# Attention scores as plain float32 products of four heads on their own 32 rows

## Chip, cores and metric

The kernel runs on one core of a Trainium2 chip, in one launch. The metric is the device time of that core in microseconds. A profile is one execution taken by the hardware profiler; its span runs from the first to the last instruction.

## What is computed

The input is one sequence of 2048 tokens of width 448, with 16 heads of 28. Two attention layers run on the same tokens and a gate mixes them. Layer A is a linear attention with learned feature maps; layer B is full softmax attention, and the change lies in B.

```python
# layer B, per head, Dh = 28
scores = einsum("bhqd,bhkd->bhqk", q, k) * Dh ** -0.5
p = softmax(scores, axis=-1)
o = einsum("bhqk,bhkd->bhqd", p, v)
b = merge_heads(o) @ wo
# x = A_x for both layers
g = sigmoid((x * gate_w).sum(-1, keepdims=True))
out = g * a + (1 - g) * b
```

## The kernel before

**Stages.** The kernel first makes the projections (q and k of layer B go through `keep_qk` to a scratch tensor `qk_d` in HBM), then layer A, then the values of layer B, and from about a third of the time on the attention of B, step by step. The orders on TensorE (PE), VectorE (DVE), ScalarE (ACT) and GpSimd (POOL) are those written in the code. The order of the DMAs on the SP queue is laid out by the framework, and each DMA waits for the one eight before it besides its own data.

**Two floats for one.** A float32r product is one TensorE instruction and keeps fewer bits than float32. `keep_qk` therefore writes a pair for each q and k: index 0 the rounded value, made by ACT (L571), and index 1 the remainder, made by DVE from the first (L572). A score tile stacks them on the rows of the array: `load_stack` puts four blocks of 28 rows into 128 partitions, q as (high, high, low, low), k as (high, low, high, low), so that one float32r product over 128 rows gives the whole score. Each tile holds four heads side by side in its free dimension.

**The maximum.** The exponential needs a maximum for each query. Row 0 of the key stack holds -1 and row 0 of the query stack holds the query's maximum, so the subtraction is done within the product. The maxima are found ahead by visits (`mx_visit`): four heads at a time, each a float32r product of its 28 rows of high parts in its own 32 rows of the array (`tile_position=(32 * j, 0)`), written to four PSUM banks. ACT copies one of the four out (`rl`, L325), DVE reduces the others (L329, L332, L335). A finished maximum lies in `nm`, and `load_nm` copies it into row 0 of the query stack by DMA.

**The attention.** There are 4 groups of four heads, 4 blocks of 512 queries, and 16 tiles of 128 keys: 256 steps `s`. Each step issues, in this order, the scores of step s for four heads (`scores`, L850, tiles `st`), the values of step s-1 (`values`, L977, four heads in four column tiles of 32, plain float32, accumulated in `pv`), and, in the first 212 steps, one visit (L321, tiles `pm`). ACT makes four exponentials a step (L868, `p<-st`), then `rl`. At the end of a query block `finish` normalizes; with the last group of heads an output projection (`project`, L988) falls into four steps of a block.

**The PSUM banks.** Seven banks rotate through a list `free`, an eighth holds `pv`. `scores` takes four from the head of the list. After both halves of the scores the list is laid out anew, `a` being the four score banks of this step and `m` the three that the last visit held for DVE:

```python
free.extend([a[0], m[0], a[1], m[1], a[2], a[3], m[2]] if m else a)
```

`mx_banks` then takes the first four of them, gives the first (the one that `rl` reads) back to the end of the list at once, and holds the other three. So in a step with a visit the four score banks are, in the order of the heads: two read by the last exponentials of the step before, one read by DVE in an earlier visit, and the one read by `rl` of the visit before. When the visits are over, six banks rotate and one is kept for the projections.

**The stacks.** There are two query stacks `qst` and five key stacks `kst`, 128 x 4 x 512 each, cleared by POOL before the attention starts (L817, L819). The last block's earlier heads (`load_out`) are loaded into a key stack that is no longer used.

Of the kernel before, what the change touches and what calls it, by code (L numbers as in the profile page):

```python
# [8 lines left out]
F32 = mybir.dt.float32  # L9
F32R = mybir.dt.float32r  # L10
U32 = mybir.dt.uint32
AF = mybir.ActivationFunctionType
# [5 lines left out]
P = 128  # L18
# [3 lines left out]
DH = 28  # L22
GW = 112
NG = 4
NT = S // P
NQ = S // 512
SCALE = DH ** -0.5
# [7 lines left out]
def f32(ap):  # L35
    return ap.bitcast(F32)
# [3 lines left out]
def gated_mix_kernel(ctx, tc, xT, wqkB, wvB, wvA, wkAT, wqAT, phi, woA, woB,  # L40
# [7 lines left out]
    nc = tc.nc  # L48
# [12 lines left out]
    def ps_s(nm):  # L61
        return ps.tile([P, 512], F32, tag="s", name=nm, bufs=psn[0])
# [13 lines left out]
    q_d = [qk_d[g * GW:(g + 1) * GW] for g in range(NG)]  # L76
    k_d = [qk_d[D + g * GW:D + (g + 1) * GW] for g in range(NG)]
# [40 lines left out]
    def tok_major(dst, t, w, n, mid=None):  # L118

        todo = [(x, w[:, i, b, :n]) for b, x, i in x3(slice(t * P, (t + 1) * P))]  # L120
        if mid is None:
            run(dst[:, :n], todo)
            return
        for i, (l, r) in enumerate(todo):
            mid(i)
            nc.tensor.matmul(dst[:, :n], l, r, start=i == 0, stop=i == len(todo) - 1,  # L126
                             skip_group_check=True)
# [36 lines left out]
    def take_acts():  # L164
        while acts:
            acts.pop(0)()
# [401 lines left out]
    def keep_qk(m, t, pq, ev):  # L568
        tt = slice(t * 512, (t + 1) * 512)
        e = ev.tile([P, 2, 512], F32R, tag="ev", name=f"ev{t}_{m}")  # L570
        nc.scalar.copy(e[:, 0, :], pq)  # L571
        nc.vector.tensor_sub(e[:, 1, :], pq, f32(e[:, 0, :]))  # L572
        nc.sync.dma_start(qk_d[m * P:(m + 1) * P, :, tt], f32(e))


# [115 lines left out]
    def value_b(t, mid=None):  # L691
        pv = ps_s(f"pvb{t}")
        tok_major(pv, t, wvB_s, D, mid)
        nc.scalar.copy(vb[t // 8][:, t % 8, :, 0:DH], pv[:, :D].rearrange("p (h d) -> p h d", d=DH))  # L694
# [11 lines left out]
    for i in range(2 * NT + 11):  # L706
        t, q = i, i - NT
# [31 lines left out]
        if 0 <= q < NT:  # L739
            pq = ps_s(f"pq{q}")  # L740
# [69 lines left out]
    at = ctx.enter_context(tc.tile_pool(name="at", bufs=1, side="right", reuse_waits="tile"))  # L810
    qst_of, kst_of = {}, {}
# [1 line left out]


    def stack(nm, keys):
        r = at.tile([P, 4, 512], F32R, name=nm)
        nc.gpsimd.memset(f32(r), 0.0)  # L817
        if keys:
            nc.gpsimd.memset(f32(r[0:1]), -1.0)  # L819
        return r  # L820

    def load_stack(r, src, c, parts):
        for b, i in enumerate(parts):
            nc.sync.dma_start(f32(r[32 * b + 4:32 * b + 32]),
                              src[:, i, c:c + 512].rearrange("(j d) n -> d j n", d=DH))
        return r

    def load_q(gq):
        g, qb = divmod(gq, NQ)
        qst_of[gq] = load_stack(qst[gq % 2], q_d[g], qb * 512, (0, 0, 1, 1))  # L830

    def load_nm(gq):
        nm = nm_of.pop(gq)
        row = f32(qst_of[gq][0:1].rearrange("p a (t b r) -> p (a t) b r", b=4, r=32))
        for b in range(4):
            nc.sync.dma_start(row[:, :, b, :], nm[32 * b:32 * b + 16, :])

    def load_k(g, kb):
        kst_of[(g, kb)] = load_stack(kst[(4 * g + kb) % 5], k_d[g], kb * 512, (0, 1, 0, 1))

    NS = NG * NQ * NT
    pv_of, pts, late, mids = {}, {}, {}, {}

    def scores(s, i):

        gq, kt = divmod(s, NT)
        g, qb = divmod(gq, NQ)

        def score(j, st):
            nc.tensor.matmul(st, kst_of[(g, kt // 4)][:, j, (kt % 4) * P:(kt % 4 + 1) * P],  # L850
                             qst_of[gq][:, j, :], start=True, stop=True)

        if s == 0:
            p = at.tile([P, 2, 512], F32, name=f"p{s}_{i}")
            st = ps_mx(f"st{s}_{i}", i)
            for jl in range(2):
                score(2 * i + jl, st[:, jl, :])
            nc.scalar.activation(p, st, AF.Exp, scale=SCALE)
            pts.setdefault(s, []).extend([p[:, 0, :], p[:, 1, :]])
            return  # L860
        sts = []
        for j in (2 * i, 2 * i + 1):
            used.append(free.pop(0))
            sts.append(bank(used[-1], f"st{s}_{j}"))
            score(j, sts[-1])
        for st in sts:
            p = late_p.tile([P, 512], F32, tag="p", name=f"p{s}_{len(pts.get(s, []))}", bufs=8)
            nc.scalar.activation(p, st, AF.Exp, scale=SCALE)  # L868
            pts.setdefault(s, []).append(p)
        if i == 1:  # L870
            a, m = used[:], held[:]
            free.extend([a[0], m[0], a[1], m[1], a[2], a[3], m[2]] if m else a)
            used.clear()
            held.clear()

    qst = [stack("qst0", False)]
    kst = [stack(f"kst{i}", True) for i in range(5)]
# [10 lines left out]
    for t in range(8, NT):  # L888


        if t < NT - 1:
            value_b(t, lambda i: mx_unit() if (11 * (t - 8) + i + 1) * rest // 77
                    > (11 * (t - 8) + i) * rest // 77 else None)
        else:
            value_b(t, lambda i: scores(0, i // 3 - 1) if i in (4, 7) else None)
        take_acts()
        if t in (8, 12):
            load_k(0, t // 12)
# [9 lines left out]
    free, used, held = list(range(7)), [], []  # L908
    spare = []

    def bank(i, nm):
        return ps2.tile([P, 512], F32, tag=f"g{i}", name=nm, bufs=1)
# [17 lines left out]
    def load_out(qb):  # L930


        if qb < NQ - 1:
            o = late_p.tile([P, NG - 1, 2, 512], F32R, tag="oL", name=f"oL{qb}", bufs=1)
            oL_of[qb] = [o[:, b] for b in range(NG - 1)]
        else:
            o = kst[(4 * NG) % 5]
            oL_of[qb] = [o[:, 0:2], o[:, 2:4],
                         late_p.tile([P, 2, 512], F32R, tag="oLl", name="oLl", bufs=1)]
        tt = slice(qb * 512, (qb + 1) * 512)  # L940
        for b in range(2):
            nc.sync.dma_start(f32(oL_of[qb][b]), o_d[b * P:(b + 1) * P, :, tt])
        r = oL_of[qb][2]
        for i in range(2):
            nc.sync.dma_start(f32(r[:80, i, :]), o_d[256:336, 0, tt])
        nc.sync.dma_start(f32(r[80:, 0, :]), o_d[288:336, 1, tt])
        nc.sync.dma_start(f32(r[80:96, 1, :]), o_d[288:304, 1, tt])
        nc.sync.dma_start(f32(r[96:, 1, :]), o_d[256:288, 1, tt])
# [145 lines left out]
    for s in range(NS + 16):  # L1094
        take_acts()
        if s < NS:
            gq, kt = divmod(s, NT)
            g, qb = divmod(gq, NQ)
            if s in (0, 3):
                load_k(0, 2 + s // 3)  # L1100
            if g + 1 < NG and qb == NQ - 1 and kt % 4 == 2:
                load_k(g + 1, kt // 4)
            if kt == 12 and gq + 1 < NG * NQ:
                load_q(gq + 1)
            if kt == (12 if gq + 1 < 14 else 14) and gq + 1 < NG * NQ - 1:
                load_nm(gq + 1)
            if s in OUTS:
                load_out(OUTS.index(s))
            if g == NG - 1 and kt == 8:
                load_acc(qb)  # L1110
            if s:
                scores(s, 0)
                scores(s, 1)
        if s == NS:
            tail_open()
            tail_fill(3)
        if 0 < s <= NS:
            values(s - 1)
            if s % NT == 0:
                finish(s // NT - 1, s)  # L1120
        if s:
            mx_visit()
        if mxs["f"] == len(flats):
            mx_fin()
        if s in mids:
            mids.pop(s)()
        if mxs["f"] == len(flats) and not spare:
            spare_open()
        if NG * NQ - 1 in nm_of and NG * NQ - 1 in qst_of:
            load_nm(NG * NQ - 1)  # L1130
        for fn in late.pop(s, []):
            fn()
# [68 lines left out]
```

## Time and profile before

| | |
|---|---|
| time, median of 2 runs | 1028.54 us (1028.19 to 1028.88) |
| span of the profiled execution | 1027.1 us |
| PE busy | 1018.7 us, 99% |
| ACT busy | 819.4 us, 80% |
| DVE busy | 672.8 us, 65% |
| POOL busy | 245.1 us, 24% |
| DMA | 98.88 MB, mean 96 GB/s |
| granted TensorE clock | 0.998 |

The profiled execution's own time is its span and what lies around it; the median of the runs is 1.4 us above the span. In the rows below, a line names engine, source line and operation, the tile written and the tiles read, then sizes and count. PE stands for matmuls, PEld for the weight loads ahead of them, SPq for the DMA issues. Groups show busy time, mean nanoseconds of one, then the idle time of the engine ahead of them and what ended it. A timeline row begins with the start and the length of the group in us. A row of the windows view has each engine's busy time and the number of its instructions in that stretch, in the order PE, PEld, DVE, ACT, POOL. Matmul ends are modelled, so starts are the better measure.

### The profile page before, as it was taken

The page shows a single profiled execution, that of the slowest core. Times are in us where ns is not written, and L with a number is a line of the kernel's source. Part 1 is how long each engine was busy: PE and PEld are TensorE (multiplying, and loading weights), DVE is VectorE, ACT ScalarE, POOL GpSimd, SP SyncE. Part 2 cuts the span into 40 slices and gives each one's busy share as a digit, 9 for nine tenths or more (in the row PEclk, how much of TensorE's full clock was granted, in tenths as well). Part 3 has the DMA queues.
Part 4 walks back from the last instruction along what each step waited for, and adds up shares of the span by engine and source line. Part 5 has one row for each costly group of instructions (what it writes and reads, how often), then busy time and mean ns, then how long its engine had stood idle before and what let it go on. Part 6 is the DMA issues. An engine that isn't in the chain of part 4 may idle for free.

```text
span 1027.1 us, 17751 instructions
## 1 busy us (share of the span) xinstructions
PE 1018.7 (99%) x6344; PEld 561.2 (55%) x6344; DVE 672.8 (65%) x1335; ACT 819.4 (80%) x1534; POOL 245.1 (24%) x213
## 2 busy tenths in 40 slices
PE   8999999999999999999999999999999999999998
PEld 7878888878779433333333333333333333354545
DVE  5466566997750578888878788787878887710102
ACT  5354445687753899999999999999999999969672
POOL 1226456688436302111011110101201101011010
PEclk9999999999999999999999999999999999999999
DMA  8873110132245703233633123522313355414311
GB/s 294 292 243 116 42 34 19 43 90 79 91 129 122 158 19 83 65 71 68 127 70 77 46 66 81 129 57 50 87 46 74 87 131 138 124 56 127 122 42 54
DMA packets 64025, 98.88 MB, mean 96 GB/s; under 512 B 17952, under 2 KB 24720, under 8 KB 63936
## 3 DMA queue, kind: packets, MB, share of 16 engines
q1 hardware_dynamic: 63936, 97.74, 35.4%
q8 instruction: 50, 0.82, 0.4%
q14 instruction: 39, 0.32, 0.1%
HBM read 69.54 MB, written 27.78 MB: 95 GB/s over the span
## 4 chain that ended last, share of the span: by engine, by line
PE 95%; DVE 2%; DMA 1%; ACT 1%; issue 0%; SPq 0%; DVEq 0%; ACTq 0%
PE st L850 29%; PE pv L977 25%; PE pm L321 9%; PE pqk L108 5%; PE poa L108 4%; PE pk L126 4%; PE pva L126 4%; PE pob L108 3%; PE pq L108 3%; PE pvb L108 2%; PE pmb L284 2%; PE pvb L126 2%; PE pn L532 1%; PE pft L520 1%; PE pkv L475 1%; PE poL L1011 1%
## 5 line engine op out<-in xcount | busy, mean ns | idle before, releaser
L868 ACT ACTIVATE p<-st 128x512 f32<-128x512 f32 x1020 | 525.9, 609 | 29.5 <-PE st L850 27.8
L332 DVE TENSOR_REDUCE part<-pm 128x1 f32<-128x512 f32 x477 | 304.6, 685 | 131.5 <-PE pm L321 124.9
L850 PE MATMUL st<-qst,kst 128*128 128x512 f32 x1024 | 315.6, 430 | 0.5 <-ACT vb L694 0.5
L977 PE MATMUL pv<-p,vb 128*32 128x512 f32 x2048 | 272.8, 605 | 0.2 <-DVE oUb L398 0.2
L850 PEld LDWEIGHTS st<-qst,kst 128*128 128x128 f32 x1024 | 173.1, 187 | 137.4 <-issue 75.8
L321 PEld LDWEIGHTS pm<-kc,qc 28*128 28x128 f32 x848 | 40.5, 181 | 177.8 <-ACT p L868 169.4
L325 ACT ACTIVATE rl<-pm 128x512 f32<-128x512 f32 x212 | 126.9, 599 | 11.1 <-PE pm L321 0.3
L419 POOL TENSOR_TENSOR oUb<-oUb,rsb 128x512 f32<-128x512 f32 x15 | 19.4, 1291 | 469.2 <-DMA rsb<-rdb 375.1
L329 DVE CUSTOM_DVE_ANT_0 rl<-pm,rl 128x512 f32<-128x512 f32 x159 | 108.2, 680 | 0.0
L321 PE MATMUL pm<-kc,qc 28*128 28x512 f32 x848 | 107.1, 495 | 0.0
L289 DVE CUSTOM_DVE_ANT_0 rl<-pmb,rl 128x512 f32<-128x512 f32 x88 | 57.1, 686 | 32.4 <-ACT rl L287 32.4
L977 PEld LDWEIGHTS pv<-p,vb 128*32 128x32 f32 x2048 | 40.3, 108 | 67.6 <-issue 63.4
L988 DVE SCALAR_TENSOR_TENSOR acc<-pob,gate,acc 128x448 f32<-128x448 f32 x12 | 8.2, 683 | 86.2 <-PE pob L108 86.2
L108 PE MATMUL pqk<-XH,wB 128*128 128x512 f32 x192 | 60.8, 404 | 2.3 <-DVE ev L572 2.3
L287 ACT ACTIVATE rl<-pmd 128x1024 f32<-128x1024 f32 x44 | 45.3, 1029 | 8.0 <-ACT z_s L485 2.4
L571 ACT CAST ev<-pqk 128x512 fp32r<-128x512 f32 x28 | 16.0, 589 | 40.2 <-PE pqk L108 35.7
L108 PE MATMUL poa<-woA_s,oTa 128*128 128x448 f32 x192 | 43.2, 374 | 0.0
L108 PEld LDWEIGHTS pqk<-XH,wB 128*128 128x128 f32 x192 | 36.0, 192 | 11.4 <-DVE ev L572 2.7
L572 DVE TENSOR_TENSOR ev<-pqk,ev 128x512 fp32r<-128x512 f32 x28 | 19.0, 690 | 31.6 <-ACT ev L571 31.5
L108 PEld LDWEIGHTS poa<-woA_s,oTa 128*128 128x128 f32 x192 | 35.0, 188 | 5.8 <-issue 2.8
L195 POOL TENSOR_TENSOR kc<-kc,kd 28x512 fp32r<-28x512 f32 x12 | 15.4, 1282 | 95.7 <-DMA kc<-qkd 59.4
L126 PE MATMUL pk<-wkA_s,XH 128*128 128x448 f32 x128 | 37.9, 377 | 0.0
(155 smaller groups left out, 1186.6 us busy)
## 6 DMA issues: line engine op xcount, KB each, us to landing
qkd<-ev SPq DMA_DIRECT2D x28, 512.0 KB
qst<-qkd SPq DMA_DIRECT2D x64, 224.0 KB
kst<-qkd SPq DMA_DIRECT2D x64, 224.0 KB
od<-oTb SPq DMA_DIRECT2D x48, 112.0 KB
rsa<-rda SPq DMA_DIRECT2D x8, 512.0 KB
rsb<-rdb SPq DMA_DIRECT2D x15, 256.0 KB
kc<-qkd SPq DMA_DIRECT2D x64, 56.0 KB
gad<-ga SPq DMA_DIRECT2D x16, 224.0 KB
```

What stands on the lines that cost most here:

```text
L108: nc.tensor.matmul(dst, l, r, start=i == 0, stop=i == len(todo) - 1)
L126: nc.tensor.matmul(dst[:, :n], l, r, start=i == 0, stop=i == len(todo) - 1, skip_group_check=True)
L284: nc.tensor.matmul((pb if j < 2 else pd)[:, j % 2, :], qc[js, qt * P:(qt + 1) * P], kc[js, :], start=True, stop=True, tile_position=(32 * ...
L287: nc.scalar.activation(rl, pd, AF.Relu)
L289: nc.vector.tensor_tensor_reduce(rl[:, i, :], pb[:, i, :], rl[:, i, :], 1.0, LOWEST, ALU.add, ALU.max, part[:, col + i:col + i + 1])
L321: nc.tensor.matmul(pm[j], mxs[("qc", gq)][js, qt * P:(qt + 1) * P], mxs[("kc", g, kb)][js, :], start=True, stop=True, tile_position=(32 * ...
L325: nc.scalar.activation(rl, pm[kb], AF.Relu if kb < 3 else AF.Copy)
L329: nc.vector.tensor_tensor_reduce(r, pm[j], r, 1.0, LOWEST, ALU.add, ALU.max, part[:, col + j:col + j + 1])
L332: nc.vector.tensor_reduce(part[:, col + j:col + j + 1], pm[j], AX.X, ALU.max)
L850: nc.tensor.matmul(st, kst_of[(g, kt // 4)][:, j, (kt % 4) * P:(kt % 4 + 1) * P], qst_of[gq][:, j, :], start=True, stop=True)
L868: nc.scalar.activation(p, st, AF.Exp, scale=SCALE)
L977: nc.tensor.matmul(pv[32 * j:32 * j + 32, :], vb[kt // 8][:, kt % 8, 4 * g + j, :], pt[j], start=kt == 0, stop=kt == NT - 1, tile_position ...
```

## The change

The scores become plain float32 products. Each head has its 28 rows (and the row of the maximum) in its own 32 rows of the array, in the tiling that the maxima have, and there are no low parts: index 1 of the pair in `qk_d` now holds the whole float32 value, and the stacks load that alone. The stacks shrink to 128 x 512; the row of -1 and the row of maxima stand in four partitions instead of one, so that `load_nm` issues 16 DMAs instead of 4. `scores` handles a step's four heads in one call instead of two calls of two heads. Step 0's scores stand at one place in the last value tile instead of two, and the last block's loads get a tile of their own.

```diff
@@ keep_qk
-        nc.vector.tensor_sub(e[:, 1, :], pq, f32(e[:, 0, :]))
+        nc.vector.tensor_copy(f32(e[:, 1, :]), pq)
@@ stack, load_stack, load_q, load_nm, load_k
-        r = at.tile([P, 4, 512], F32R, name=nm)
-        nc.gpsimd.memset(f32(r), 0.0)
+        r = at.tile([P, 512], F32, name=nm)
+        nc.gpsimd.memset(r, 0.0)
         if keys:
-            nc.gpsimd.memset(f32(r[0:1]), -1.0)
+            for e in range(0, P, 32):
+                nc.gpsimd.memset(r[e:e + 1], -1.0)
         return r
 
-    def load_stack(r, src, c, parts):
-        for b, i in enumerate(parts):
-            nc.sync.dma_start(f32(r[32 * b + 4:32 * b + 32]),
-                              src[:, i, c:c + 512].rearrange("(j d) n -> d j n", d=DH))
+    def load_stack(r, src, c):
+        for j in range(4):
+            nc.sync.dma_start(r[32 * j + 4:32 * j + 32], src[DH * j:DH * j + DH, 1, c:c + 512])
         return r
...
-        row = f32(qst_of[gq][0:1].rearrange("p a (t b r) -> p (a t) b r", b=4, r=32))
-        for b in range(4):
-            nc.sync.dma_start(row[:, :, b, :], nm[32 * b:32 * b + 16, :])
+        for j in range(4):
+            row = qst_of[gq][32 * j:32 * j + 1].rearrange("o (t b r) -> o t b r", b=4, r=32)
+            for b in range(4):
+                nc.sync.dma_start(row[:, :, b, :], nm[32 * b + 4 * j:32 * b + 4 * j + 4, :])
@@ scores
-    def scores(s, i):
+    def scores(s):
...
-            nc.tensor.matmul(st, kst_of[(g, kt // 4)][:, j, (kt % 4) * P:(kt % 4 + 1) * P],
-                             qst_of[gq][:, j, :], start=True, stop=True)
+            rows = slice(32 * j, 32 * j + 32)
+            nc.tensor.matmul(st, kst_of[(g, kt // 4)][rows, (kt % 4) * P:(kt % 4 + 1) * P],
+                             qst_of[gq][rows], start=True, stop=True, tile_position=(32 * j, 0))
...
-        sts = []
-        for j in (2 * i, 2 * i + 1):
-            used.append(free.pop(0))
-            sts.append(bank(used[-1], f"st{s}_{j}"))
-            score(j, sts[-1])
+        a = [free.pop(0) for _ in range(4)]
+        sts = [bank(a[j], f"st{s}_{j}") for j in range(4)]
+        for j in range(4):
+            score(j, sts[j])
         for st in sts:
             p = late_p.tile([P, 512], F32, tag="p", name=f"p{s}_{len(pts.get(s, []))}", bufs=8)
             nc.scalar.activation(p, st, AF.Exp, scale=SCALE)
             pts.setdefault(s, []).append(p)
-        if i == 1:
-            a, m = used[:], held[:]
-            free.extend([a[0], m[0], a[1], m[1], a[2], a[3], m[2]] if m else a)
-            used.clear()
-            held.clear()
+        m = held[:]
+        free.extend([a[0], m[0], a[1], m[1], a[2], a[3], m[2]] if m else a)
+        held.clear()
@@ the value tile of step 0
-            value_b(t, lambda i: scores(0, i // 3 - 1) if i in (4, 7) else None)
+            value_b(t, lambda i: scores(0) if i == 7 else None)
@@ load_out
-            o = kst[(4 * NG) % 5]
+            o = at.tile([P, 4, 512], F32R, name="oLs")
@@ the steps
-                scores(s, 0)
-                scores(s, 1)
+                scores(s)
```

More of the change, by code (lines that the diff above doesn't have):

```diff
@@ L829, in load_q @@
         g, qb = divmod(gq, NQ)
-        qst_of[gq] = load_stack(qst[gq % 2], q_d[g], qb * 512, (0, 0, 1, 1))
+        qst_of[gq] = load_stack(qst[gq % 2], q_d[g], qb * 512)
     def load_nm(gq):
         nm = nm_of.pop(gq)
-        row = f32(qst_of[gq][0:1].rearrange("p a (t b r) -> p (a t) b r", b=4, r=32))
-        for b in range(4):
-            nc.sync.dma_start(row[:, :, b, :], nm[32 * b:32 * b + 16, :])
+        for j in range(4):
+            row = qst_of[gq][32 * j:32 * j + 1].rearrange("o (t b r) -> o t b r", b=4, r=32)
+            for b in range(4):
+                nc.sync.dma_start(row[:, :, b, :], nm[32 * b + 4 * j:32 * b + 4 * j + 4, :])
     def load_k(g, kb):
-        kst_of[(g, kb)] = load_stack(kst[(4 * g + kb) % 5], k_d[g], kb * 512, (0, 1, 0, 1))
+        kst_of[(g, kb)] = load_stack(kst[(4 * g + kb) % 5], k_d[g], kb * 512)
     NS = NG * NQ * NT
     pv_of, pts, late, mids = {}, {}, {}, {}
-    def scores(s, i):
+    def scores(s):
         gq, kt = divmod(s, NT)
@@ L849, in score @@
         def score(j, st):
-            nc.tensor.matmul(st, kst_of[(g, kt // 4)][:, j, (kt % 4) * P:(kt % 4 + 1) * P],
-                             qst_of[gq][:, j, :], start=True, stop=True)
+            rows = slice(32 * j, 32 * j + 32)
+            nc.tensor.matmul(st, kst_of[(g, kt // 4)][rows, (kt % 4) * P:(kt % 4 + 1) * P],
+                             qst_of[gq][rows], start=True, stop=True, tile_position=(32 * j, 0))
         if s == 0:
[L854 to L859, printed above, removed]
-            return
-        sts = []
-        for j in (2 * i, 2 * i + 1):
-            used.append(free.pop(0))
-            sts.append(bank(used[-1], f"st{s}_{j}"))
-            score(j, sts[-1])
+            st = [ps_mx(f"st{s}_{k}", k) for k in range(2)]
+            for j in range(4):
+                score(j, st[j // 2][:, j % 2, :])
+            for k in range(2):
+                p = at.tile([P, 2, 512], F32, name=f"p{s}_{k}")
+                nc.scalar.activation(p, st[k], AF.Exp, scale=SCALE)
+                pts.setdefault(s, []).extend([p[:, 0, :], p[:, 1, :]])
+            return
+        a = [free.pop(0) for _ in range(4)]
+        sts = [bank(a[j], f"st{s}_{j}") for j in range(4)]
+        for j in range(4):
+            score(j, sts[j])
         for st in sts:
```

## The prediction

> **What bounds the kernel now.** I read the page first (span, busy shares, chain), then the attention stage by windows, then one step of it in the timeline, then the waits of the scores' line.
>
> ```profile
> span 1027.1 us, 17751 instructions
> PE 1018.7 (99%) x6344; PEld 561.2 (55%) x6344; DVE 672.8 (65%) x1335; ACT 819.4 (80%) x1534; POOL 245.1 (24%) x213
> PE st L850 29%; PE pv L977 25%; PE pm L321 9%; PE pqk L108 5%; PE poa L108 4%; PE pk L126 4%; PE pva L126 4%; PE pob L108 3%; PE pq L108 3%; PE pvb L108 2%; PE pmb L284 2%; PE pvb L126 2%; PE pn L532 1%; PE pft L520 1%; PE pkv L475 1%; PE poL L1011 1%
> L868 ACT ACTIVATE p<-st 128x512 f32<-128x512 f32 x1020 | 525.9, 609 | 29.5 <-PE st L850 27.8
> L850 PE MATMUL st<-qst,kst 128*128 128x512 f32 x1024 | 315.6, 430 | 0.5 <-ACT vb L694 0.5
> L977 PE MATMUL pv<-p,vb 128*32 128x512 f32 x2048 | 272.8, 605 | 0.2 <-DVE oUb L398 0.2
> L325 ACT ACTIVATE rl<-pm 128x512 f32<-128x512 f32 x212 | 126.9, 599 | 11.1 <-PE pm L321 0.3
> ```
>
> TensorE is never idle and carries the chain: scores 29%, values 25%, maxima 9%. There are 256 attention steps (1024 score products, four a step); 212 of them also hold a visit of the maxima (212 `rl`). The values are 2048 instructions for 1024 calls: a plain float32 product is two instructions here, the float32r score is one. The change will make 2048 out of 1024. Now the stage with visits, and one step in it:
>
> ```profile
> 342.50:890.00 547.50, 547.50 (x3364) 214.28 (x3360) 443.09 (x891) 536.57 (x1050) 56.63 (x54) 1.00 0.35 83
> ...
> 701.93 0.51 PE L321 MATMUL pm<-kc,qc 28*128 28x512 f32 x4
> 702.36 0.53 PEld L850 LDWEIGHTS st<-qst,kst 128*128 128x128 f32 x3 [0.24 <-issue]
> 702.36 1.25 PE L850 MATMUL st<-qst,kst 128*128 128x512 f32 x4
> 702.46 0.60 ACT L325 ACTIVATE rl<-pm 128x512 f32<-128x512 f32 x1
> 702.96 2.06 ACT L868 ACTIVATE p<-st 128x512 f32<-128x512 f32 x4
> 703.11 0.19 PEld L850 LDWEIGHTS st<-qst,kst 128*128 128x128 f32 x1 [0.22 <-ACT rl L325]
> 703.54 0.16 PEld L977 LDWEIGHTS pv<-p,vb 128*32 128x32 f32 x8 [0.24 <-issue]
> 703.54 1.06 PE L977 MATMUL pv<-p,vb 128*32 128x512 f32 x8
> 704.53 0.51 PE L321 MATMUL pm<-kc,qc 28*128 28x512 f32 x4
> 705.07 0.60 ACT L325 ACTIVATE rl<-pm 128x512 f32<-128x512 f32 x1
> ```
>
> By window ACT is busy 536.57 of 547.50 us, PE all of it: two full engines, so the order of waits decides. From one start to the next, TensorE's slots are pm 0.43 (701.93 to 702.36), st 1.18 (to 703.54), pv 0.99 (to 704.53): 2.60. But look at the fourth weight load of the scores: alone, at 703.11, held by `rl`. The scores' line says how often:
>
> ```profile
>   ACT rl L325: 46.1, 212
> ```
>
> All 212 visits. The reason is in the code: the fourth score bank of a step is the bank that `rl` of the visit before reads. So a loop closes through both engines: `rl` runs 0.60 (702.46 to 703.06), 0.05 later the fourth weights load (703.11), 0.43 later pv starts (703.54), 0.99 later pm (704.53), 0.54 later the next `rl` (705.07). Sum 2.61, the step exactly. Whatever lengthens the fourth score product lengthens the step by as much.
>
> **The change, part by part.** Scores first. Afterwards a head's product is two float32 instructions of 512 columns on 32 rows, four heads side by side. No row shows that; the bounds come from pv (two float32 rounds, four tiles wide, by columns) and pm (one round, four tiles by rows, the same 128-column weights):
>
> ```profile
> 703.53:703.90 0.37, 0.36 (x4) 0.16 (x8) 0.00 (x0) 1.00 0.53 155
> 703.90:704.10 0.20, 0.20 (x8) 0.00 (x0) 0.00 (x0) 1.00 0.32 82
> L977 PE MATMUL pv<-p,vb x2048: 592/605/617, 341.2 to 1012.3; 128*32 128x512 f32 x187
> L850 PEld LDWEIGHTS st<-qst,kst x1024: 186/187/192, 336.9 to 1009.4; 128*128 128x128 f32 x171
> L977 PEld LDWEIGHTS pv<-p,vb x2048: 106/108/109, 341.2 to 1011.8; 128*32 128x32 f32 x187
> ```
>
> Restricted to pv, the windows show four matmuls under way until 703.90 and eight after it, with all eight weights loaded at once: two rounds of four. The group ends 1.06 after its start and a late matmul takes 0.59, so the second round starts 0.47 after the first. Two rounds plus weights and the switch to the next tiling fill the 0.99 slot. Scores have 128-column weights instead of 32, which take 187 against 108 ns: add 0.08, slot 1.07. From pm: its 0.43 holds one float32r round; replacing that (half of a 0.43 to 0.45 float32 round) by two gives 0.43 - 0.22 + 0.88 = 1.09. I take 1.07.
>
> The four heads cannot all use it together. Heads 0 to 2 wait for the last two exponentials of the step before and for a VectorE reduce, all done by then; in the changed program's order head 3 still waits on ScalarE, and the bank list still gives it `rl`'s bank. It starts after `rl`, when the other three are well on, and runs its two rounds nearly alone: 1.07 from its weights to pv, where now it is 0.43. Queued behind that wait are pv, pm and the next `rl`. New step: 0.60 + 0.05 + 1.07 + 0.99 + 0.54 = 3.25, so +0.64, times 212 = **+136 us**. Bounds for head 3: 0.97 if the other heads' tiles let its weights load ahead (+0.54 a step, +114), 1.26 if the second round's weights are not loaded under the first (+0.83, +176). The nearest row, pv's eight early loads, speaks for neither, so 1.07 stays.
>
> The Trainium skill has a rule here, in "TensorE: Matmul & The Clock Gate", Part 3 (packing small matmuls): products in different row groups run at once and a pack lasts about one matmul plus 4 ns for each further tile. By it alone the st slot falls from 1.18 to 1.07, or -0.11 x 212 = -23 us; by the row of 212 waits the fourth tile is not there when the pack starts, and the sum is +136.
>
> The 43 steps after the last visit (256 less 213), 12 of them with an output projection (12 `acc`):
>
> ```profile
> 929.24 1.19 PE L850 MATMUL st<-qst,kst 128*128 128x512 f32 x4
> 930.36 1.06 PE L977 MATMUL pv<-p,vb 128*32 128x512 f32 x8
> 931.36 0.76 PEld L850 LDWEIGHTS st<-qst,kst 128*128 128x128 f32 x4 [0.84 <-issue]
> ...
> 911.53 0.77 PE L108 MATMUL pob<-woB_s,oTb 128*128 128x448 f32 x3
> 912.14 1.09 PE L850 MATMUL st<-qst,kst 128*128 128x512 f32 x4
> 913.16 1.06 PE L977 MATMUL pv<-p,vb 128*32 128x512 f32 x8
> L988 DVE SCALAR_TENSOR_TENSOR acc<-pob,gate,acc 128x448 f32<-128x448 f32 x12 | 8.2, 683 | 86.2 <-PE pob L108 86.2
> ```
>
> Now 2.12 a step. Six banks rotate, so head 3 takes the bank that the second exponential of the step before frees. After the change heads 0 to 2 are done 0.96 after st starts, the first exponential starts 0.2 later, the second 0.48 after it (four in 2.06, the last 0.63) and ends after 0.60: 2.25. With P the step, head 3 starts at 2.25 + 0.05 - P, and 0.96 + 0.11 + 0.99 later the next st starts: P = 2.18, +0.06 x 31 = +2 us. After a projection there is no such wait, but the untiled weights that used to load under the projection now follow a switch: about 1.07 + 0.1 against 1.02 (912.14 to 913.16), +0.15 x 12 = +2 us.
>
> Small things, one answer together. The SP queue:
>
> ```profile
> 323.44 1.65 SPq L824 DMA_DIRECT2D qst<-qkd  x4
> 325.13 2.53 SPq L836 DMA_DIRECT2D qst<-nm  x4
> 327.76 13.16 SPq L824 DMA_DIRECT2D kst<-qkd  x16
> ```
>
> Loads of `qst` and `kst` stay four each and move a quarter of the bytes; the maxima's row goes from 4 to 16 DMAs, 0.63 each: 7.6 us more per query block, against 16 steps of 3.25. In the changed program's order they stand one block ahead of their use, bar the first block: there the first keys are issued behind them at about 335 instead of 327.8, and the first scores ran at 336.88. With about 2 us to land, up to +1.5; value 1. The `ev` edit:
>
> ```profile
> L572 DVE TENSOR_TENSOR ev<-pqk,ev 128x512 fp32r<-128x512 f32 x28 | 19.0, 690 | 31.6 <-ACT ev L571 31.5
> L398 DVE COPY oUb<-pv 128x512 f32<-128x512 f32 x15 | 10.4, 691 | 16.4 <-PE pv L977 9.7 <-PE st L850 6.0 <-PE pm L321 0.7
> PEld pqk L108 <- DVE ev L572: 2.7, 1, 2.7
> ```
>
> A copy costs what the subtraction does (691 against 690) but need not wait for ScalarE; TensorE waited for it 2.7 us once. Between 0 and -3; I take -1. At the very end the last pv waits for its fourth exponential, +0.4. The memsets are POOL work under the projections: 0, and if that cover is gone under 2.
>
> Sum against the profiled execution: 1027.1 + 136 + 2 + 2 + 1 - 1 + 0.4 = 1167.5 us of span. The median of the runs, 1028.54, is 1.4 above that span, so the time is **1169 us**.
>
> **The rivals.**
> *The pack is whole (faster).* Place: head 3 of a step. If its wait does not hold (its product takes 0.43 or less from its weights, or the bank is free before st starts), TensorE's slots sum to 1.07 + 0.99 + 0.43 = 2.49, -23 us; and since pm and st would have one tiling, the switch and weights between them (0.2) may go too. Then ScalarE is the bound with (2.06 - 0.63) / 3 = 0.48 for each of five instructions, 2.41: -0.20 x 212 = -42. Between them, **996 us**. For it: scores are the largest share of the chain. Against: the 212 waits. It decides from the point where rl's end to pv is under 0.48.
>
> *The two halves of a head run one after the other, and the next head's first half only beside the second (slower still).* Four heads would take five rounds of 0.43. From pm's start: 0.43, then 2.15, 0.11, 0.99: 3.68, +1.07 x 212 = +227; without visits +1.25 x 43 = +54: **1310 us**. Against it stand pv's two rounds in 0.99. The same part of the Trainium skill says matmuls start and end in strict program order, which would give this case if the halves are issued head by head. By that rule pv would take five rounds, too, and its row says two.
>
> *Nothing moves (same).* Head 3's longer product would have to hide behind the wait that is there already. The loop has no slack: its five terms make up the 2.61 exactly. **1030 us**.
>
> **How the numbers follow.** 0.84 for the forecast, 0.07 for the whole pack, 0.06 for the five rounds, 0.03 for nothing. Head 3's bounds give 1027.1 + 114 + 4 + 1.4 = 1147 and 1027.1 + 176 + 5 + 1.4 = 1210; the upper one is the less likely, so the range is 1145 to 1205. The other cases lie outside it, with 0.16. A measurement of this kernel can tell about 2% from no change: faster 0.07, same 0.03, slower 0.90.
>
> **What would show it.** In the profile after: st with 2048 matmuls; a step with a visit of 3.25 us; ScalarE at 2.5 of 3.25, about three quarters, and idle before `p` on the scores; one weight load in each visit step released by `rl`, now followed by pv after 1.07; the same 0.99 for pv and 0.54 from pm to `rl`; 2.2 in the steps without a visit. Wrong is the forecast if the fourth load is no longer held by `rl`, if it is followed by pv within 0.5, or if st's eight matmuls spread over more than three rounds.

## The result and the profile after

The changed kernel takes 1165.1 us (median of 2 runs, 1164.71 to 1165.48) against 1028.54 us: 1.133 times the time before (95% interval 1.1295 to 1.1361). The forecast was 1169 us in a range of 1145 to 1205. Three of the six executions of E8 below and one of the four of E9 ran at a mean granted clock of 0.67 and took 1325 to 1328 us; the times given for these two are those of the others. The page of the changed kernel, with the span, the engines, the chain and the groups that answer to those quoted of before:

```profile
span 1163.7 us, 20186 instructions
PE 1154.3 (99%) x7368; PEld 552.4 (47%) x7368; DVE 673.2 (58%) x1335; ACT 841.9 (72%) x1534; POOL 237.1 (20%) x228
PE st L852 37%; PE pv L977 22%; PE pm L321 8%; PE pqk L108 5%; PE poa L108 4%; PE pk L126 3%; PE pva L126 3%; PE pob L108 3%; PE pq L108 2%; PE pvb L108 2%; PE pvb L126 1%; PE pmb L284 1%; PE pn L532 1%; PE pft L520 1%; PE pkv L475 1%; PE poL L1011 1%
L870 ACT ACTIVATE p<-st 128x512 f32<-128x512 f32 x1020 | 526.9, 602 | 90.9 <-PE st L852 90.9
L852 PE MATMUL st<-qst,kst 32*128 32x512 f32 x2048 | 471.6, 617 | 0.4 <-ACT vb L694 0.4
L977 PE MATMUL pv<-p,vb 128*32 128x512 f32 x2048 | 272.9, 605 | 0.0
L325 ACT ACTIVATE rl<-pm 128x512 f32<-128x512 f32 x212 | 126.6, 597 | 63.4 <-PE pm L321 63.4
```

The scores are 2048 matmuls and 37% of the chain instead of 29%. TensorE still counts as busy for 99% of the span. That figure hides what happened: a matmul that is under way alone, with three of the four row tiles empty, counts as busy too (in the step below only head 3's, from 702.83 to 703.64). The idle time of ScalarE ahead of the exponentials says it better: 90.9 us, all of it spent on scores, against 29.5 before. Next, one step of the attention in the timeline (start, length, line, tiles, count; the bracket is the engine's idle time and what ended it), and the wait of the scores' weight loads for `rl` (us, times):

```profile
701.41 0.51 PE L321 MATMUL pm<-kc,qc 28*128 28x512 f32 x4
701.52 0.47 PEld L852 LDWEIGHTS st<-qst,kst 32*128 32x128 f32 x6
701.75 1.96 PE L852 MATMUL st<-qst,kst 32*128 32x512 f32 x8
701.94 0.60 ACT L325 ACTIVATE rl<-pm 128x512 f32<-128x512 f32 x1 [0.30 <-PE pm L321]
702.59 0.29 PEld L852 LDWEIGHTS st<-qst,kst 32*128 32x128 f32 x2 [0.60 <-ACT rl L325]
702.81 2.06 ACT L870 ACTIVATE p<-st 128x512 f32<-128x512 f32 x4 [0.27 <-PE st L852]
703.64 1.07 PE L977 MATMUL pv<-p,vb 128*32 128x512 f32 x8
704.64 0.50 PE L321 MATMUL pm<-kc,qc 28*128 28x512 f32 x4
705.17 0.60 ACT L325 ACTIVATE rl<-pm 128x512 f32<-128x512 f32 x1 [0.30 <-PE pm L321]
  ACT rl L325: 122.5, 209
```

Six of the eight weight loads of a step (heads 0 to 2, two instructions each) begin at 701.52, under the maxima. The other two, head 3's, stand alone at 702.59, behind `rl`. Read the loop from `rl` to `rl`: 0.60, then 0.05 to head 3's weights, 1.05 to pv (703.64), 1.00 to pm (704.64), 0.53 to the next `rl`: 3.23 us. Before it was 2.61, and the link from head 3's weights to pv was 0.43.

By stages, from starts in the trace: the first pv is 0.74 us later; from there to the pv of the 212th step it takes 681.3 instead of 550.0 us (+131.3); from there to the last pv 125.1 instead of 120.6 (+4.5, of which 0.62 is the one step with a visit that is left); the rest differs by 0.1. Together +136.6, the difference of the two spans. The windows of the two stages (busy time of PE, PEld, DVE, ACT and POOL, then granted clock, DMA share and GB/s):

```profile
342.50:1021.00 678.50, 678.50 (x4208) 219.73 (x4200) 443.10 (x891) 559.93 (x1053) 55.18 (x53) 1.00 0.15 40
1021.00:1146.00 125.00, 125.00 (x840) 49.52 (x836) 15.11 (x28) 89.91 (x175) 9.51 (x9) 1.00 0.23 72
```

VectorE has the same work in the first window as before (443.10 against 443.09 us), spread over 131 us more.

### The profile page after: what moved, and what is told of

Same layout as the page of the kernel before. It is cut to its first block, busy times and chain, and to the rows that moved or that the text cites. A ratio compares the mean times of both kernels' runs of the same rounds, so it can differ in the third digit from the quotient of the medians.

```text
span 1163.7 us, 20186 instructions
## 1 busy us (share of the span) xinstructions
PE 1154.3 (99%) x7368; PEld 552.4 (47%) x7368; DVE 673.2 (58%) x1335; ACT 841.9 (72%) x1534; POOL 237.1 (20%) x228
## 4 chain that ended last, share of the span: by engine, by line
PE 96%; DVE 2%; DMA 1%; ACT 1%; issue 0%; SPq 0%; DVEq 0%; ACTq 0%
PE st L852 37%; PE pv L977 22%; PE pm L321 8%; PE pqk L108 5%; PE poa L108 4%; PE pk L126 3%; PE pva L126 3%; PE pob L108 3%; PE pq L108 2%; PE pvb L108 2%; PE pvb L126 1%; PE pmb L284 1%; PE pn L532 1%; PE pft L520 1%; PE pkv L475 1%; PE poL L1011 1%
## 5 line engine op out<-in xcount | busy, mean ns | idle before, releaser
L870 ACT ACTIVATE p<-st 128x512 f32<-128x512 f32 x1020 | 526.9, 602 | 90.9 <-PE st L852 90.9
L852 PE MATMUL st<-qst,kst 32*128 32x512 f32 x2048 | 471.6, 617 | 0.4 <-ACT vb L694 0.4
L852 PEld LDWEIGHTS st<-qst,kst 32*128 32x128 f32 x2048 | 183.0, 183 | 154.8 <-ACT rl L325 122.5
L108 PE MATMUL pq<-wqA_s,XH 128*128 128x448 f32 x128 | 37.4, 374 | 0.0
```

Of the source, the lines that this page charges most:

```text
L108: nc.tensor.matmul(dst, l, r, start=i == 0, stop=i == len(todo) - 1)
L852: nc.tensor.matmul(st, kst_of[(g, kt // 4)][rows, (kt % 4) * P:(kt % 4 + 1) * P], qst_of[gq][rows], start=True, stop=True, tile_position=( ...
```

## The experiments

The theory: head 3 of a step waits for the bank that `rl` reads, and its whole product then lies alone on the loop through `rl`. The main rivals: the plain float32 pack is slow in itself, whatever waits; or TensorE's slots add up to 3.2 us with no loop.

**E1: `rl` twice as long.** ScalarE reads the bank a second time into a spare tile, and nothing else is added.

```diff
             nc.scalar.activation(rl, pm[kb], AF.Relu if kb < 3 else AF.Copy)
+            rl2 = late_p.tile([P, 512], F32, tag="rl2", name=f"rl2_{f}", bufs=1)
+            nc.scalar.activation(rl2, pm[kb], AF.Relu if kb < 3 else AF.Copy)
```

> The changed kernel with rl made twice by ScalarE in every visit (the second copy goes to a tile that nothing reads), so that its bank comes free one ScalarE instruction (0.48 us) later. Theory (the loop rl, head 3, pv, pm, rl sets the step): step 3.23 + 0.48 = 3.71 us, so 1165 + 0.48 x 212 = 1267 us (1255 to 1280). Rival (the step is longer because two rounds per head are more TensorE work, and the wait on rl only lies beside it): ScalarE has 3.23 - 5 x 0.48 = 0.8 us to spare in each step, the second copy fits in, 1165 us (1160 to 1175).

Measured: 1268.9 us (one run; the kernel before on the same chip 1027.15). One step of it in the timeline:

```profile
703.79 0.60 ACT L325 ACTIVATE rl<-pm 128x512 f32<-128x512 f32 x1 [0.67 <-PE pm L321]
704.28 0.59 ACT L327 ACTIVATE rl<-pm 128x512 f32<-128x512 f32 x1
704.92 0.29 PEld L854 LDWEIGHTS st<-qst,kst 32*128 32x128 f32 x2 [1.13 <-ACT rl L327]
705.98 0.16 PEld L979 LDWEIGHTS pv<-p,vb 128*32 128x32 f32 x8 [0.76 <-issue]
```

The second copy starts 0.49 us after the first, head 3's weights move back by as much, and pv follows them after 1.06 again. The step becomes 3.72 us (median), +0.49. ScalarE was idle for 0.30 + 0.27 us of each step in the changed kernel, more than the 0.49 added, and none of it took up the copy: `rl` lies on the loop.

**E2: the same rows, one instruction for a product.** The heads keep their own 32 rows and the bank list stays as it is, but a product is one float32r instruction.

```diff
-        r = at.tile([P, 512], F32, name=nm)
-        nc.gpsimd.memset(r, 0.0)
+        r = at.tile([P, 512], F32R, name=nm)
+        nc.gpsimd.memset(f32(r), 0.0)
...
-            nc.sync.dma_start(r[32 * j + 4:32 * j + 32], src[DH * j:DH * j + DH, 1, c:c + 512])
+            nc.sync.dma_start(f32(r[32 * j + 4:32 * j + 32]), src[DH * j:DH * j + DH, 0, c:c + 512])
```

> The changed kernel with its scores as float32r products of the high parts alone, on the same 32 rows for each head; the low parts are left out, so the scores keep fewer bits. One instruction per head instead of two. Theory: head 3 takes 0.43 us from its weights to pv again, the loop is 0.60 + 0.05 + 0.43 + 0.99 + 0.54 = 2.61 us, the step of before, though TensorE has much less to do (pm 0.32, st 0.43, pv 0.99, 1.75 in all); visits give 1165 - 0.62 x 212 = 1034, the 43 later steps some 16 less: 1018 us (1010 to 1032). Rival (sum of TensorE's work): the step falls to ScalarE's 5 x 0.48 = 2.41, 1165 - 0.82 x 212 - 16 = 975 us (965 to 990).

Measured: 1017.0 us (one run, before 1027.15). Its head 3 in the timeline:

```profile
701.84 0.18 PEld L852 LDWEIGHTS st<-qst,kst 32*128 32x128 f32 x1 [0.40 <-ACT rl L325]
702.26 0.16 PEld L977 LDWEIGHTS pv<-p,vb 128*32 128x32 f32 x8 [0.24 <-issue]
703.26 0.51 PE L321 MATMUL pm<-kc,qc 28*128 28x512 f32 x4
```

The wait for `rl` is still there, but pv follows the late weights after 0.42, and the step is 2.60, the old one. The tiling, the one call for four heads, the sixteen DMAs of the row and the bank order are all in this kernel, and its step is no longer than before. What costs is the second instruction of a product, and the rows show it at head 3.

**E3 and E4: no visits.** The visits' matmuls, copies and reduces are left out, of the changed kernel (E3) and of the kernel before (E4); the maxima that they would have found stay 0.

```diff
-            pm = mx_banks(f, kb)
-            for j in sorted(range(4), key=lambda j: j != kb):
...
-            rl = late_p.tile([P, 512], F32, tag="rl", name=f"rl{f}", bufs=3)
-            nc.scalar.activation(rl, pm[kb], AF.Relu if kb < 3 else AF.Copy)
...
-                    nc.vector.tensor_reduce(part[:, col + j:col + j + 1], pm[j], AX.X, ALU.max)
```

> The changed kernel without the visits' products, copies and reductions in the attention steps (their loads stay, those maxima are 0); all seven banks serve the scores for 212 steps. Theory: with banks enough the row tiling costs nothing: st 1.07 + pv 0.99 = 2.07 us a step, up to 2.18 where pv waits for the last exponential: 1165 - (1.05 to 1.16) x 212 = 919 to 942 us, 931 likeliest, within 2% of the same cut of the kernel before. Rival (two rounds per head are more TensorE work): only the visit's own 0.43 goes, 3.23 - 0.43 = 2.80 a step, 1074 us.

> The kernel before with the same cut (no products, copies and reductions of the visits in the attention steps). Both theories: st 1.13 + pv 0.99 = 2.12 us a step, as in its steps without visits, 1028.5 - 0.49 x 212 = 925 us (918 to 935). It is the yardstick for the cut changed kernel.

Measured: 941.0 us for E3 and 939.3 us for E4 (one run each). Both lie above the likeliest forecast, E4 outside its range. E3's steps are uneven (2.16 us in the mean). E4's are 2.12, but where the heads change, three took 6.14, 3.82 and 5.42 us and two of their neighbours 3.24 and 2.80. In the longest, TensorE waited for the next keys, of which this kernel loads four times as many bytes:

```profile
480.03 1.59 PE L831 MATMUL st<-qst,kst 128*128 128x512 f32 x4 [3.55 <-DMA kst<-qkd]
```

These five steps hold 10.8 us more than five of 2.12. So the plain difference, 1.7 us instead of 137, flatters the change: in the steps themselves it costs some 12 us without visits. That is still less than a tenth of the loss. In E3's timeline all eight weight loads go together:

```profile
700.96 0.31 PEld L833 LDWEIGHTS st<-qst,kst 32*128 32x128 f32 x8 [0.84 <-issue]
702.03 0.16 PEld L958 LDWEIGHTS pv<-p,vb 128*32 128x32 f32 x8 [0.76 <-issue]
703.03 0.31 PEld L833 LDWEIGHTS st<-qst,kst 32*128 32x128 f32 x8 [0.84 <-issue]
```

The whole pack of four heads takes 1.07 us from its weights to pv; the old scores take 1.12 without visits (E4, 701.61 to 702.73). So the first rival, a pack that is slow in itself, is out. The second, slots that add up to 3.2 us with no loop, is out by E1, where TensorE's work was the same and the step longer.

**E5: a visit without `rl`.** A visit does three heads, which VectorE reduces; the fourth and `rl` are left out, and the list of banks is laid out in another order.

```diff
-            pm = mx_banks(f, kb)
+            b = [free.pop(0) for _ in range(3)]
+            held.extend(b)
+            for n, j in enumerate(sorted({0, 1, 2, 3} - {kb})):
+                pm = bank(b[n], f"pm{f}_{j}")
...
-            nc.scalar.activation(rl, pm[kb], AF.Relu if kb < 3 else AF.Copy)
...
-        free.extend([a[0], m[0], a[1], m[1], a[2], a[3], m[2]] if m else a)
+        free.extend([a[0], m[0], m[1], m[2], a[1], a[2], a[3]] if m else a)
```

> The changed kernel with visits of three heads: the head that rl reads is left out with its bank and with rl (its maxima stay 0), and DVE reduces the other three straight from PSUM. Seven banks then hold the four scores and three maxima of a step. Theory: no score waits on rl any more; head 3 waits for the fourth exponential of the step before instead, and the step is 2.65 to 2.85 us: 1165 - (0.38 to 0.58) x 212 = 1042 to 1084 us, 1063 likeliest. Rival (TensorE's work): three maxima side by side last as long as four and the scores keep their two rounds, so the step stays within 0.1 of 3.23: 1144 to 1165 us.

Measured: 1075.3 us (before on the same chip 1027.15), 90 us below the changed kernel. Most steps alternate between 2.29 and 3.33 us, and the mean is 2.81. From two neighbours:

```profile
701.46 1.95 PE L842 MATMUL st<-qst,kst 32*128 32x512 f32 x8
702.28 0.29 PEld L842 LDWEIGHTS st<-qst,kst 32*128 32x128 f32 x2 [0.20 <-ACT p L860]
703.34 0.16 PEld L967 LDWEIGHTS pv<-p,vb 128*32 128x32 f32 x8 [0.76 <-issue]
704.35 0.74 PEld L842 LDWEIGHTS st<-qst,kst 32*128 32x128 f32 x8
```

In the first, one head is late again, now for a bank that an exponential reads, and pv follows 1.06 after it. In the next all eight loads go at once. Who the late reader is does not matter; that there is one does.

**E6: the waiting head first.** If a late head 3 finds the array empty and runs alone, one could let all heads wait. Head 0 gets `rl`'s bank, so that the other three stand behind it.

```diff
         a = [free.pop(0) for _ in range(4)]
+        if held:
+            a = [a[3], a[0], a[1], a[2]]
```

> The changed kernel with the score banks dealt out in another order: head 0 gets the bank that rl reads, heads 1 to 3 the others. Same instructions, same banks. Theory: TensorE issues in order, so all four heads now start after rl; the four exponentials of a step start together with the end of head 3, and ScalarE (0.21 + 4 x 0.48 + 0.60 to the end of the next rl) joins the loop: 2.73 + 0.05 + 0.96 = 3.74 us a step, 1165 + 0.51 x 212 = 1273 us (1240 to 1290). Rival (TensorE's work alone): the order of the banks does not matter, 1165 us (1160 to 1175).

Measured: 1296.8 us, above the range of the theory by 7 and far from the rival. A step of it at full clock:

```profile
602.32 0.31 PEld L852 LDWEIGHTS st<-qst,kst 32*128 32x128 f32 x8 [1.29 <-ACT rl L325]
603.39 0.16 PEld L979 LDWEIGHTS pv<-p,vb 128*32 128x32 f32 x8 [0.76 <-issue]
```

From the released weights to pv it is 1.07 us for four heads, and it was 1.05 for one: a late head costs as much as a late pack. The step is 3.77 us (median) and 3.85 in the mean: in eight short stretches the clock was down, and the 16 steps that they touch took 4.0 to 5.4 us, 14 us above the median together, which the forecast did not have (last section). Without them it would lie within the range.

**E7: a visit in two parts.** The head that `rl` reads goes ahead of the scores, the other three between scores and values. Each product takes the bank that is due first, by times set ahead in the code for a step of 2.69 us. Now no score has to wait for the `rl` just before it.

```diff
+            pm = {}
+            head(kb, 1.18)
             rl = late_p.tile([P, 512], F32, tag="rl", name=f"rl{f}", bufs=3)
             nc.scalar.activation(rl, pm[kb], AF.Relu if kb < 3 else AF.Copy)
-            for j in sorted({0, 1, 2, 3} - {kb}, key=lambda j: j == kb - 1):
+            yield
+            rest = sorted({0, 1, 2, 3} - {kb}, key=lambda j: j == kb - 1)
+            for n, j in enumerate(rest):
+                head(j, (2.2, 2.8, 3.5)[n])
...
-        a = [free.pop(0) for _ in range(4)]
+        a = [free.take(s, off) for off in (2.2, 2.7, 3.1, 3.6)]
...
+            i = min(self.due, key=self.due.get)
+            self.due[i] = 2.69 * s + off
...
@@ the steps
+            visit = mx_visit(s) if s else iter(())
+            next(visit, None)
             if s:
                 scores(s)
+                next(visit, None)
```

> The changed kernel in another order, nothing left out: in each step the head of the visit that rl reads goes first, then the step's four scores, then the other three heads of the visit, then pv; ScalarE makes rl ahead of the exponentials; the bank that is due to come free first is taken next. Theory: rl is done long before any score needs its bank, so the loop through rl is cut; what is left is that seven banks hold eight products, and a score still waits for an exponential or a reduction of the step before: 2.6 to 2.85 us a step, 1165 - (0.38 to 0.63) x 212 = 1031 to 1084 us, 1053 likeliest, so much faster than the changed kernel and not clearly faster than the one before. Rival (TensorE's work): the same products in another order, 1165 us (1150 to 1175).

Measured: 1054.32 us (1052.82 to 1056.19, 4 runs), 1.0248 times the kernel before (95% interval 1.0225 to 1.0271) and 111 us below the changed kernel. One step, and the end of the next:

```profile
700.36 0.75 PEld L861 LDWEIGHTS st<-qst,kst 32*128 32x128 f32 x8
701.41 0.30 PEld L321 LDWEIGHTS pm<-kc,qc 28*128 28x128 f32 x3 [0.31 <-DVE part L336]
702.10 0.16 PEld L988 LDWEIGHTS pv<-p,vb 128*32 128x32 f32 x8 [0.38 <-issue]
703.09 0.50 PE L321 MATMUL pm<-kc,qc 28*128 28x512 f32 x1
703.67 0.63 ACT L328 ACTIVATE rl<-pm 128x512 f32<-128x512 f32 x1
704.35 0.18 PEld L321 LDWEIGHTS pm<-kc,qc 28*128 28x128 f32 x1 [0.18 <-ACT rl L328]
704.77 0.16 PEld L988 LDWEIGHTS pv<-p,vb 128*32 128x32 f32 x8 [0.25 <-issue]
```

The eight loads of the scores form one group again. But the loop through `rl` is not gone. Seven banks serve eight products a step, and by the times in the code the last of the three maxima gets the bank with the earliest one (1.18), which `rl` of the same visit reads. In 210 of the 212 visits its weights load 0.05 us after `rl` ends, as at 704.35 above. What comes late is now a maximum, one instruction, and pv follows its weights after 0.43 (median) instead of 1.05. The five terms are 0.60, 0.05, 0.43, 1.00 and 0.54 in the medians, 2.62, and the median step is 2.61, that of the kernel before. So E7 confirms E2 from the other side: the loop costs what the late product lasts. That its forecast of 1053 us came out is partly luck, since it had the loop cut.

The mean step is 2.71. In one step of 8.56 us VectorE waited 5.5 us for a DMA, and the granted clock was at half behind it (last section); with its neighbour that makes 7.6 us of the 25 that E7 loses to the kernel before. Some 47 steps of 2.75 to 2.90 and the steps after the visits (+4.2) are the larger part of the rest.

**E8, E9 and E10: can the one-instruction version be improved?** E9 is E2 once more, over several rounds. E8 joins E2 with the split visit of E7, the due times of the banks set for a step of 2.46 (shown against E7). E10 is E8 once more, for a profile.

```diff
-            self.due[i] = 2.69 * s + off
+            self.due[i] = 2.46 * s + off
```

> The scores go on the heads' own 32 rows, but as float32r products of the high parts alone (low parts left out, fewer bits), and the visit is split: the head of the maxima that rl reads goes ahead of the scores, the other three behind them, banks by the order in which they come free. Theory (the step of the single-product version, 2.60 us, is the loop of rl through the fourth score bank): with the visit split the loop is gone and ScalarE bounds the step, five instructions of about 0.49 us each, 2.46 us; 212 x (2.604 - 2.46) = 31 us less than 1017.0: 986 us (980 to 1015, since the split of the plain float32 version left its steps uneven by 0.1 us on average). Rival (the step of 2.60 is TensorE's slots and not the loop): 1010 to 1025 us.

> The single-product version (float32r products of the high parts on the heads' own 32 rows, low parts left out, the visit whole), once more and against the kernel before in several rounds. Theory (the loop through rl is the same length as before, since head 3 holds 0.43 us again; only the 43 steps without a visit and the projection steps are shorter): 1017 us, 0.99 of before. Rival (the single run's 1% was chance): a ratio whose interval holds 1.

Measured: E9 1017.4 us (1017.0 to 1018.4), 0.9886 times the kernel before (95% interval 0.9869 to 0.9902). E8 1016.6 us (1015.6 to 1017.1), 0.9871 (0.9851 to 0.9891). E9 confirms E2: 1.1% under the kernel before, a small difference but outside the noise, at the price of the low parts. Nearly all of it lies in the steps after the visits (110.2 us against 120.6); the steps with visits stay at 2.60. E8 is not told apart from E9: none of the 31 us came that its theory had forecast. Why was the question of E10:

> The split visit with single float32r products (high parts alone, low parts left out) for its steps: its time, 1016 us, equals that of the whole visit, 1017 us, so the loop through rl is gone or not, and something else holds 2.6 us. Theory one: three weight loads a step still wait on ScalarE or VectorE, in another place (the two parts of the visit each wait for a bank), with idle gaps on TensorE's weight side between the packs; median step 2.6 with one part of the maxima released by rl or a reduce. Theory two: TensorE's slots fill 2.6 us without a wait, since the maxima need two slots where they needed one (0.43 + 0.3).

E10 took 1325.9 us, and TensorE's clock was granted at half in nearly all of the steps with visits (last section), so its steps of 4.06 us say nothing on their length at full clock. The order of the waits can be read all the same:

```profile
1191.93 0.60 ACT L328 ACTIVATE rl<-pm 128x512 f32<-128x512 f32 x1 [1.50 <-PE st L861]
1192.58 0.28 PEld L321 LDWEIGHTS pm<-kc,qc 28*128 28x128 f32 x1 [0.97 <-ACT rl L328]
1193.29 0.20 PEld L988 LDWEIGHTS pv<-p,vb 128*32 128x32 f32 x8 [0.43 <-issue]
1195.16 0.28 PEld L321 LDWEIGHTS pm<-kc,qc 28*128 28x128 f32 x1 [1.66 <-ACT p L879]
1195.99 0.60 ACT L328 ACTIVATE rl<-pm 128x512 f32<-128x512 f32 x1 [1.50 <-PE st L861]
```

The last maximum waits for `rl`, as in E7, and in all 212 visits. The terms 0.60, 0.05, 0.71, 1.87 and 0.83 make up the 4.06. So E8's theory failed at its premise: the split did not cut the loop, it put one product of one instruction in the place of another. At full clock E7's terms would give 2.62, an estimate, and E9's step is 2.60; that fits the equal times, but no profile of E8 at full clock shows it.

## Why the prediction was right, point by point

- **Head 3 from its weights to pv.** Predicted 1.07 (bounds 0.97 and 1.26), measured 1.05. E2 halves the instructions of a product and measures 0.42; E6 shows 1.07 for a whole pack from its release. The reasoning from pv's two rounds carried over to row tiles, and to a head that runs its two halves nearly alone (0.53 and 0.52).
- **The loop.** Its five terms were predicted as 0.60, 0.05, 1.07, 0.99 and 0.54; they are 0.60, 0.05, 1.05, 1.00 and 0.53. The step grew by 0.62 instead of 0.64, which is 132 us in 212 visits instead of 136, and nearly all of the miss of 3.9 us in the total. E1 shows that the loop sets the step, E2 and E7 that the late product's length counts in full, E3 and E5 that it needs `rl` or another late reader.
- **Steps without a visit.** Predicted 2.18, measured 2.20 in the mean, but not evenly. These are weight loads of the scores in five such steps of the changed kernel:

```profile
1060.74 0.58 PEld L852 LDWEIGHTS st<-qst,kst 32*128 32x128 f32 x8 [0.84 <-issue]
1063.07 0.31 PEld L852 LDWEIGHTS st<-qst,kst 32*128 32x128 f32 x8 [0.84 <-issue]
1065.14 0.58 PEld L852 LDWEIGHTS st<-qst,kst 32*128 32x128 f32 x8 [0.84 <-issue]
1067.47 0.31 PEld L852 LDWEIGHTS st<-qst,kst 32*128 32x128 f32 x8 [0.84 <-issue]
1069.54 0.58 PEld L852 LDWEIGHTS st<-qst,kst 32*128 32x128 f32 x8 [0.84 <-issue]
```

  They come 2.33, 2.07, 2.33 and 2.07 apart. Where the loads last 0.58 instead of 0.31 the pack is stretched. The prediction's recurrence gave one number for all of them; the mean was right, the pattern was not foreseen. The steps with a projection grew by 0.14 (predicted 0.15), and the end as a whole by 3.9 without the last step with a visit (predicted 4).
- **Small things.** The first pv came 0.74 us later. Predicted were +1 from the sixteen DMAs of the row and -1 from the copy, so the sum was near but its parts were not shown. The copy did not end the wait that it was to end: TensorE's weights waited for `ev` 3.2 us once, after 2.7 before. The first keys were issued at 333.79 instead of 327.76, yet the weights of the first scores load at 337.27 instead of 336.88, and the profile names no DMA in the 0.31 us of waiting ahead of them.
- **A sign against it.** More than three rounds of st's eight matmuls were to speak against the forecast. By their starts there are four: 701.75, 702.18 to 702.24, 702.59 and 703.13. The late head's first half overlaps the second halves of the others by some 0.2 us and has no round in common with them. The sign was set too narrowly; the time of the late head came as forecast.
- **ScalarE's share.** Predicted three quarters of a step; the window says 559.93 of 678.50, or 83%. The step of the timeline gives it: 2.06 for the four exponentials and 0.60 for `rl` are 2.66 of 3.23, where the prediction had counted 2.5. It bore on no term of the sum.
- **The rivals.** The whole pack needed the wait for `rl` to be gone, and it was there in 209 of the 212 visits. Whether 996 us can be reached without it stays open, since no run here has a step with a full visit and no late product. Five rounds are out: E3's pack of four heads takes 1.07 us, in two rounds 0.53 apart. (The sum of that rival has a slip: by its own terms a step without a visit would be 2.15 + 0.11 + 0.99 = 3.25, +1.13 and not +1.25, which makes some 5 us less.) The Trainium skill's rule that matmuls start and end in strict program order ("TensorE: Matmul & The Clock Gate", Part 3) would give the five rounds if the halves are issued head by head. It does not describe plain float32 products in separate tiles here, in whichever order they are issued: at 1063.07 all four first halves of the changed kernel start ahead of any second half, while at 702.18 three second halves start ahead of head 3's first, 702.59, and the code of both steps is the same. The Trainium skill's rule on the length of a pack, in the same part, is one matmul plus about 4 ns for each further tile. It agrees with E3 round by round: four matmuls of 0.69 us last 0.71 together, and four of 0.59 last 0.61. In the changed kernel the pack was not whole, and that rule says nothing on such a pack.

## What to carry to other kernels

Before a product is made longer, look for the weight load that stands apart from its group and ask what releases it: if it closes a loop through another engine, the whole added length is paid on every turn, however small the slot's own sum is. A pack on row tiles is as late as its last PSUM bank, so order the banks by their readers' ends, or give the late bank to the shortest product; here this took back 111 of 137 us. Follow such a change through the bank list to its end: the late bank goes to some product. A busy share of 99% is no sign that an engine is full when its tiles can be empty.

## What was not expected of the hardware

In E6, TensorE is idle for part of each step, waiting for `rl`. Eight times its granted clock fell to half for 6.8 us (the last six 122.9 us apart). Two neighbouring windows of E6, and then three of E10:

```profile
515.00:522.50 7.50, 5.56 (x40) 2.22 (x39) 3.79 (x8) 5.08 (x11) 0.00 (x0) 1.00 0.11 32
522.50:530.00 7.50, 6.81 (x33) 1.41 (x32) 2.57 (x5) 4.11 (x8) 0.00 (x0) 0.54 0.02 2
```

```profile
350.00:360.00 10.00, 9.49 (x43) 2.49 (x39) 4.38 (x8) 5.48 (x12) 0.00 (x0) 0.50 0.29 74
1190.00:1200.00 10.00, 9.50 (x48) 2.33 (x44) 5.32 (x14) 5.54 (x11) 0.00 (x0) 0.50 0.08 26
1210.00:1220.00 10.00, 10.00 (x61) 5.58 (x58) 1.37 (x2) 6.12 (x13) 0.00 (x0) 1.00 0.11 38
```

In the first pair TensorE was busy for 5.56 of 7.50 us at full clock, and no single gap between the matmuls is longer than about 1 us (0.97 in the row of E6's matmuls, 1.02 at most in the stage):

```profile
520.73 1.79 PE L852 MATMUL st<-qst,kst 32*128 32x512 f32 x8 [0.97 <-ACT rl L325]
```

The Trainium skill ("TensorE: Matmul & The Clock Gate", Part 1) puts the fall to half clock down to an idle window of about 3.4 us, and adds that short gaps between groups can also make the clock swing. Here it swung with no gap above 1.02 us, and 6.8 us is two of those windows. Longer gaps were followed by a fall as well: one of 4.47 us in E7 (6.8 us at half), and of 3.55 and 2.38 us in E4 (3.4 us each).

In E10 the half clock lasted from 342.8 to 1203.0 us, 860 us in all; the first maximum of the visits was at 339.4, the last at 1196.6. TensorE was 92 to 95% busy by its records. E8's profile shows the same 860 us. The changed kernel itself never left full clock in the attention, and E1, with TensorE busy for 92% of a stretch of its visits (603.47 of 657.50 us, 342.50 to 1000.00), did not either. So the busy share alone does not tell these kernels apart; what does was not tried.
